# Six bundles of attention behind feed-forward blocks, and TensorE's queue in source order from unit 5 on

## The chip, the cores and the metric

The kernel runs on one core of a Trainium2 chip. A core has five engines with a queue each: TensorE (PE in the profile; its weight loads are listed apart as PEld), VectorE (DVE), ScalarE (ACT), GpSimd (POOL) and SyncE (SP), which here only issues DMA transfers. Each queue is executed in order; the engines run side by side and wait for one another through semaphores. The metric is the device time of one execution in microseconds (us); less is better.

## The reference

The program computes a gated linear attention and feeds its result to a feed-forward layer. All arrays are float32, with 4 batches, 8 heads, 768 tokens and head dimension 48.

```python
mag = np.sqrt(a_re * a_re + a_im * a_im)
scale = np.minimum(mag, 0.999) / (mag + 1e-06)
a_re_n, a_im_n = (a_re * scale, a_im * scale)
...
for t in range(S):
    ar, ai = (a_re_n[:, :, t, :, None], a_im_n[:, :, t, :, None])
    new_re = ar * S_re - ai * S_im
    new_im = ar * S_im + ai * S_re
    kv = np.einsum('bhd,bhe->bhde', k[:, :, t], v[:, :, t])
    S_re, S_im = (new_re + kv, new_im)
    y[:, :, t] = np.einsum('bhd,bhde->bhe', q[:, :, t], S_re)
...
x = np.ascontiguousarray(attn_out.transpose(0, 2, 1, 3)).reshape(B * S, H * D)
a = x @ w_a
b = x @ w_b
return (a * b @ w_out).astype(np.float32)
```

The state of each head is a complex 48x48 matrix that decays by its own complex factor per row at each token; the feed-forward has 3072 rows, 384 columns in and out, and 1536 columns inside.

## The kernel before

**Units.** The tokens are cut into chunks of 128, and a unit is one chunk of two batches: 256 columns of tokens. There are 12 units, 0 to 11 (`NU`): six chunks of the first pair of batches, then six of the second. Unit 6 starts from an empty state; units 5 and 11 are the last of their pair and need not update it.

**Three stages work on three units at once.** In the window of unit w (the loop `for w in range(NU)`), TensorE does the feed-forward of unit w and the attention of unit w+1, while DVE and ACT prepare unit w+2 and, late in the window, begin unit w+3.

- `prep(u)` (lines 203 to 337) turns the decay factors into products over the chunk and scales q and k by them. Its last operations are the two products of line 312 per unit, DVE operations of 1536 elements per partition, which write the buffer `qk`. It is a generator: the window's loop draws some of its operations after each block.
- `stack(u)` (line 342) then moves `qk` by ten DMA transfers from SP into the buffer `stk` (line 352), head by head. There is one `qk` and one `stk`: the next unit's `qk` is loaded when the stacking has read it, and `stk` is written anew when the attention of the unit before has read it.
- `attn(u)` does the attention, for each of the two batches i of the unit and each group g of four heads: `scores` (line 385, four float32 products of 128x128 per group from `stk` into a PSUM tile `pm`; DVE then masks them into `am`, line 388), `transposes` (line 396, the keys turned by TensorE into a `pm`, copied by ACT into `kt`, line 400), `outputs` (line 425, which adds `v`·`am` and state·`q` in an `xp` tile; its products use a 32-column strip of the array each, four side by side), ACT's copy of `xp` into `xh` (line 429), `residual` (line 434: DVE takes what the copy lost into `xl`), and `state` (line 442, `kt`·`v` into a `pm`; DVE adds it to the state, line 449, and rescales in some units, line 453). There are two `pm`, two `am` and two `kt` buffers and one `xp`.
- The feed-forward of a unit runs over 12 blocks f of 128 inner columns. `gemm1` (line 486) makes 18 products of 256 columns for a block in one of three PSUM tiles `ab`, from `xh` and `xl` and weights split into two parts; ACT and DVE multiply the two halves and split the result (lines 494 to 497). `gemm2` (line 504) makes six products of 384 columns for a block. It follows `gemm1` by two blocks (`LAG`): in the loop of block f stands `gemm1(f)`, then, through `second()`, `gemm2(f-2)`. All these use float32r, a one-pass format, on the full array.

**What sets the order.** The programming library records the instructions in the order of the source and a scheduler then fixes each engine's queue, ahead of the run, by priority (`tc.high_priority` raises it) and by its own estimate of when an operand is ready. So the source order of the attention pieces is a wish, which the scheduler may break up. On the chip the queues are fixed.

In window w the attention generator of unit w+1 yields after each of its 18 pieces (12 in units 5 and 11). `slot()` is called twice per block, behind `gemm1` and behind `gemm2`; from block `ATTN_AT` (5 for w = 0, 6 after) to block `STACK_AT` (11 for w = 0 to 2, 10 after) each call draws one or two pieces. At block `STACK_AT` what is left is drawn, `prep(w+2)` is finished, `stack(w+2)` is issued and the next `qk` is loaded.

Of the kernel before, what the change touches and what calls it, by code (L numbers as in the profile page):

```python
# [20 lines left out]
NCH = S // C  # L21
# [25 lines left out]
EARLY = 2  # L47
WARM = 8
HB = 3
O_BUFS = 3  # L50
CONV_ON_AB = 7
NCHK = NU * G + NU + 1
# [2 lines left out]
P1_AT = 4  # L55
MOE_FIRST = 4000
ATTN_FIRST = 2000
ATTN_AT = (5, 6, 6, 6, 6)
STACK_AT = (11, 11, 11, 10, 10)


# [9 lines left out]
def tile_kernel(ctx: ExitStack, tc: tile.TileContext, a_d, qk_d, v_d, w_d, qn_d, kn_d, vn_d, an_d, out_d):  # L71
    nc = tc.nc
    vec, act, pe, sync = nc.vector, nc.scalar, nc.tensor, nc.sync
# [57 lines left out]
    def split_weights():  # L131
        for f in range(NF):
            for m, (c0, n) in enumerate(WPART):
                raw = raws[f, m]
                t = moe.tile([128, n], F32, name="o_sb", bufs=O_BUFS)
                tu = t.bitcast(U32)
# [202 lines left out]
    def load_qk(u):  # L339
        sync.dma_start(out=qk[:, :, 1, 0:2 * TOK], in_=qk_d[u])  # L340

    def stack(u, cols=None):
        n = RUN if rescaled(u % NCH) else 2 * TOK
        if cols is None:
            cols = slice(TOK if u < EARLY else 0, n)
        for h in range(H):
            r0 = h * D
            while r0 < (h + 1) * D:
                j, p = divmod(r0, 128)
                m = min((h + 1) * D - r0, 128 - p)  # L350
                d0 = 2 * (r0 - h * D)
                sync.dma_start(out=stk[d0:d0 + 2 * m, h, cols], in_=qk[p:p + m, j, :, cols])
                r0 += m
# [4 lines left out]
    def load_v(u):  # L358
        for i in range(2):
            t = vpool.tile([128, 512], F32, name="v_t")  # L360
            sync.dma_start(out=t, in_=v_d[u, i])
            v_tiles[u, i] = t
# [8 lines left out]
    def attn(u, xh, xl):  # L371

        c = u % NCH
        last = c + 1 == NCH
# [61 lines left out]
        def state(i, hg):  # L436
# [10 lines left out]
            with tc.high_priority(offset=ATTN_FIRST):  # L447
# [4 lines left out]
                if rescaled(c):  # L452
                    vec.tensor_tensor(out=uv, in0=uv, in1=sv, op=ALU.mult)

        order = [(scores, 0, 0), (scores, 0, 1), (transposes, 0, 0), (transposes, 0, 1),
                 (outputs, 0, 0), (outputs, 0, 1), (scores, 1, 0), (residual, 0, 0), (state, 0, 0), (scores, 1, 1),
                 (state, 0, 1), (transposes, 1, 0), (transposes, 1, 1), (outputs, 1, 0),
                 (outputs, 1, 1), (state, 1, 0), (residual, 1, 0), (state, 1, 1)]
        if u == 0:
            order = [(scores, 0, 0), (scores, 0, 1), (outputs, 0, 0), (outputs, 0, 1), (scores, 1, 0), (scores, 1, 1),  # L460
                     (residual, 0, 0), (outputs, 1, 0), (outputs, 1, 1), (transposes, 0, 0), (transposes, 0, 1),
                     (residual, 1, 0), (state, 0, 0), (state, 0, 1), (transposes, 1, 0), (transposes, 1, 1),
                     (state, 1, 0), (state, 1, 1)]
        for fn, i, g in order:
            if not (last and fn in (transposes, state)):
                fn(i, g)
                yield

    def pieces(u):
        return 12 if u % NCH + 1 == NCH else 18  # L470

    def new_x():
        return (moe.tile([128, NJ, TOK], F32, name="xh"), moe.tile([128, NJ, TOK], F32, name="xl"))
# [6 lines left out]
    def gemm1(f, xh, xl, ps_ab=ps_ab, moe=moe):  # L480
        ab = ps_ab.tile([128, 512], F32, name="ab")
        for m in range(2):
            n = 0
            for i in range(NJ):
                for part, xt in ((0, xh), (0, xl), (1, xh)):
                    pe.matmul(out=ab[:, m * TOK:(m + 1) * TOK],  # L486
                              lhsT=r(w_ab(f, part, m * NJ + i)),
                              rhs=r(xt[:, i, :]), start=n == 0, stop=n == 8)
                    n += 1
        h_t = moe.tile([128, TOK], F32, name="h_t")  # L490
        hh = moe.tile([128, TOK], F32, name="hh", bufs=HB)
        hl = moe.tile([128, TOK], F32, name="hl", bufs=HB)
        with tc.high_priority(offset=MOE_FIRST):
            act.copy(out=h_t, in_=ab[:, 0:TOK])  # L494
            vec.tensor_tensor(out=h_t, in0=ab[:, TOK:2 * TOK], in1=h_t, op=ALU.mult)  # L495
            act.copy(out=r(hh), in_=h_t)  # L496
            vec.tensor_tensor(out=r(hl), in0=h_t, in1=hh, op=ALU.subtract)  # L497
        return hh, hl

    def gemm2(f, hh, hl, os_):  # L500
        for tt in range(2):
            ts = slice(tt * 128, (tt + 1) * 128)
            for n, (ht, part) in enumerate(((hh, 0), (hh, 1), (hl, 0))):
                pe.matmul(out=os_[tt][:, 0:DM], lhsT=r(ht[:, ts]), rhs=r(w_t[f, 2][:, part, :]),  # L504
                          start=(f == 0 and n == 0), stop=(f == NF - 1 and n == 2))
# [107 lines left out]
    def drain(gen, ns=None):  # L613
        if gen is None:
            return
        left = ns
        for cost in gen:
            if left is not None:
                left -= cost or 0
                if left <= 0:  # L620
                    return
# [10 lines left out]
    for _ in attn(0, *x_cur):  # L632
        drain(p1, P1_A)
    pend = []

    def second():
        w2, f2, hh, hl, os2 = pend.pop(0)
        gemm2(f2, hh, hl, os2)
        if f2 == NF - 1:
            for tt in range(2):  # L640
                o_sb = moe.tile([128, DM], F32, name="o_sb", bufs=O_BUFS)
                with tc.high_priority(offset=MOE_FIRST):
                    act.copy(out=o_sb, in_=os2[tt][:, 0:DM])
                act.dma_start(out=out_d[w2, tt], in_=o_sb)

    pgen = None
    for w in range(NU):
        last = w + 1 == NU
        x_nxt = None if last else new_x()
        at = None if last else attn(w + 1, *x_nxt)  # L650
        if not last:
            load_v(w + 1)
        os_ = [ps_o.tile([128, 512], F32, name=f"o{t}") for t in range(2)]
        slots = [0, 2 * (STACK_AT[min(w, 4)] + 1 - max(ATTN_AT[min(w, 4)], 0 if w else P1_AT + 1))]
        left = [pieces(w + 1)]

        def slot():
            if at is None or f < ATTN_AT[min(w, 4)] or (w == 0 and f <= P1_AT) or not slots[1]:
                return
            n = -(-left[0] // slots[1])  # L660
            slots[1] -= 1
            for _ in range(n):
                next(at, None)
                left[0] -= 1

        for f in range(NF):
            if w == 0:
                next(ws, None)
                drain(p1, P1_F)
                if f == P1_AT:  # L670
                    drain(p1)
                    stack(1)
                    for i in range(WARM):
                        wp = ps_m.tile([128, 512], F32, name="pm")
                        pe.matmul(out=wp[:, 0:TOK], lhsT=ident, rhs=qk[:, i % NJ, 1 - i // NJ % 2, TOK:2 * TOK],
                                  start=True, stop=True)
                    load_qk(2)
                    pgen = prep(2)
            pend.append((w, f, *gemm1(f, *x_cur), os_))
            slot()  # L680
            if len(pend) > LAG:
                second()
            slot()
            if f == STACK_AT[min(w, 4)]:
                drain(at)
                if w + 2 < NU:
                    drain(pgen)
                    stack(w + 2)
                if w + 3 < NU:
                    load_qk(w + 3)  # L690
                    pgen = prep(w + 3)
            if w > 0:
                drain(pgen, 2400)
        x_cur = x_nxt
# [8 lines left out]
    vec.tensor_scalar(out=bad, in0=tot[0:1, 0:1], scalar1=128.0 * NCHK, scalar2=None, op0=ALU.not_equal)  # L703
    while pend:
        second()
    fast.close()
    with tc.If(nc.values_load(bad[0:1, 0:1], min_val=0, max_val=1) > 0):
        token_by_token()
# [55 lines left out]
```

## Time and profile before

| | |
|---|---|
| time, median of 3 runs | 699.11 us (698.85 to 699.16) |
| time of the profiled execution | 698.89 us |
| its span, first to last instruction | 697.2 us |
| mean granted TensorE clock | 0.974 |
| PE, PEld, DVE, ACT busy | 655.2, 610.8, 551.8, 308.9 us |

The page of the profile lists busy time by engine, the span in 40 slices with a busy digit each (17.4 us a slice), the chain of work that ended last, and groups of instructions by line. Other views are a timeline of one engine (start, duration, engine, line, operation, tiles, shapes, count, and in brackets idle time and what ended it), the waits (who waited for whom: total, times, longest) and busy time by stretch. A float32 product is two MATMUL records in a timeline and one instruction in an order (a transpose and a float32r product are one in both). A record's duration covers its way through the array, so records overlap; what a stretch of work costs is the distance from its first start to the start of what follows.

Until about 120 us the weights are loaded and split and the first units prepared; the blocks of a window then follow one another to the end, about 51 us a window with attention in it.

### The profile page before, as it was taken

What the parts mean: (1) busy time and instruction counts of PE and PEld (TensorE: products, weight loads), DVE (VectorE), ACT (ScalarE), POOL (GpSimd) and SP (SyncE); (2) the same over time, 40 slices, a digit from 0 to 9 for tenths busy, and PEclk for the clock granted to TensorE, in tenths of its full rate; (3) what the DMA queues carried; (4) which work ended last, traced back from release to release, by engine and by line L of the source; (5) the groups of instructions that cost most, each with busy time, mean ns of one, the idle gap of its engine ahead of it and who ended that gap; (6) DMA issues with size and microseconds to landing.
All of it is one profiled execution on the core that took longest, in us unless ns stands there. A gap on an engine that the chain in (4) does not pass through costs nothing.

```text
span 697.2 us, 14316 instructions
## 1 busy us (share of the span) xinstructions
PE 655.2 (94%) x5854; PEld 610.8 (88%) x5854; DVE 551.8 (79%) x1241; ACT 308.9 (44%) x618; POOL 5.6 (1%) x11
## 2 busy tenths in 40 slices
PE   3557999999999999999999999999999999999996
PEld 1224889899899999999999999999999999999996
DVE  5999899988888889989899898999989853232221
ACT  6357755634535445245363554535542332221221
POOL 3000000000000000000000000000000000000000
PEclk9567999999999999999999999999999999999999
DMA  8973202411414205134151340511510500400000
GB/s 312 402 291 108 79 1 54 129 55 55 128 42 130 81 28 149 60 98 129 25 160 46 102 134 1 169 67 47 145 46 2 165 25 17 106 24 2 24 1 28
DMA packets 32088, 63.94 MB, mean 92 GB/s; under 512 B 3984, under 2 KB 10640, under 8 KB 32016
## 3 DMA queue, kind: packets, MB, share of 16 engines
q1 hardware_dynamic: 28560, 58.23, 27.0%
q10 hardware_dynamic: 3456, 4.72, 1.9%
q8 instruction: 48, 0.79, 0.5%
q14 instruction: 24, 0.20, 0.1%
HBM read 39.32 MB, written 4.72 MB: 63 GB/s over the span
## 4 chain that ended last, share of the span: by engine, by line
PE 64%; DVE 27%; ACT 4%; DMA 2%; issue 1%; SPq 1%; ACTq 0%; DVEq 0%
PE ab L486 30%; PE o L504 14%; PE xp L425 6%; PE pm L385 5%; PE pm L442 4%; DVE a_t L292 3%; DVE pr L230 2%; DVE qk L312 2%; DVE h_t L495 2%; PE pm L396 2%; DVE hl L497 2%; PE pm L150 2%; DVE z L297 2%; DVE pb L260 1%; DVE z L236 1%
## 5 line engine op out<-in xcount | busy, mean ns | idle before, releaser
L486 PE MATMUL ab<-xh,w 128*128 128x256 f32 x1728 | 339.0, 285 | 0.0
L486 PEld LDWEIGHTS ab<-xh,w 128*128 128x128 f32 x1728 | 278.1, 190 | 1.8 <-issue 1.4
L486 PE MATMUL ab<-xl,w 128*128 128x256 f32 x864 | 245.1, 284 | 0.0
L486 PEld LDWEIGHTS ab<-xl,w 128*128 128x128 f32 x864 | 164.4, 190 | 0.5 <-issue 0.2
L504 PE MATMUL o<-w,hh 128*128 128x384 f32 x576 | 152.3, 344 | 0.0
L494 ACT COPY h_t<-ab 128x256 f32<-128x256 f32 x144 | 53.1, 369 | 176.9 <-PE ab L486 176.8
L495 DVE TENSOR_TENSOR h_t<-ab,h_t 128x256 f32<-128x256 f32 x144 | 60.5, 420 | 72.5 <-ACT h_t L494 72.3
L504 PEld LDWEIGHTS o<-w,hh 128*128 128x128 f32 x576 | 96.8, 190 | 3.7 <-issue 3.0
L504 PE MATMUL o<-w,hl 128*128 128x384 f32 x288 | 96.9, 336 | 0.0
L496 ACT CAST hh<-h_t 128x256 fp32r<-128x256 f32 x144 | 58.0, 403 | 81.1 <-DVE h_t L495 80.9
L497 DVE TENSOR_TENSOR hl<-h_t,hh 128x256 fp32r<-128x256 f32 x144 | 60.5, 420 | 17.5 <-ACT hh L496 17.3
L150 PE MATMUL ab<-o_sb,ident 128*128 128x384 f32 x42 | 29.1, 794 | 29.9 <-DVE o_sb L141 29.8
L385 PE MATMUL pm<-stk 128*128 128x128 f32 x384 | 54.4, 279 | 2.7 <-DMA stk<-qk 2.7
L504 PEld LDWEIGHTS o<-w,hl 128*128 128x128 f32 x288 | 54.1, 188 | 0.0
L385 PEld LDWEIGHTS pm<-stk 128*128 128x128 f32 x384 | 48.7, 191 | 5.9 <-issue 4.8
L230 DVE TENSOR_TENSOR pr<-z 128x384 f32<-128x384 f32 (+1 forms) x91 | 47.1, 524 | 2.4 <-ACT z L216 0.8
L150 PEld LDWEIGHTS ab<-o_sb,ident 128*128 128x128 f32 x42 | 10.2, 286 | 39.8 <-DVE o_sb L141 29.4
L292 DVE TENSOR_TENSOR a_t<-z,b_t 128x768 f32<-128x768 f32 x48 | 44.6, 952 | 0.1
L425 PE MATMUL xp<-am,v_t 128*32 128x128 f32 x768 | 42.5, 277 | 1.3 <-DVE am L388 1.2
L312 DVE TENSOR_TENSOR qk<-qk,z 128x1536 f32<-128x1536 f32 (+1 forms) x28 | 42.7, 1524 | 0.1
L388 DVE TENSOR_TENSOR am<-pm,mask 128x512 f32<-128x512 f32 x48 | 32.8, 685 | 5.0 <-PE pm L385 4.8
L425 PE MATMUL xp<-stk,u 128*32 128x128 f32 x640 | 34.4, 273 | 0.0
(106 smaller groups left out, 761.7 us busy)
## 6 DMA issues: line engine op xcount, KB each, us to landing
w<-in_dram SPq DMA_DIRECT2D x36, 384.0 KB, 8.1
qk<-in_dram SPq DMA_DIRECT2D x12, 768.0 KB, 4.8
a_t<-in_dram SPq DMA_DIRECT2D x11, 768.0 KB, 4.3
stk<-qk SPq DMA_DIRECT2D x42, 192.0 KB, 3.3
v_t<-in_dram SPq DMA_DIRECT2D x24, 256.0 KB, 2.7
out_dram<-o_sb ACTq DMA_DIRECT2D x24, 192.0 KB, 1.9
stk<-qk SPq DMA_DIRECT2D x18, 192.8 KB, 3.4
stk<-qk SPq DMA_DIRECT2D x14, 128.0 KB, 3.1
```

Of the source, the lines that this page charges most:

```text
L150: pe.matmul(out=lp[:, 0:n], lhsT=ident, rhs=t, start=True, stop=False)
L230: vec.tensor_tensor(out=pr[:, :, :, o:o + n], in0=view(zz, W + at_(i) + 2 * o, [[W, 2], [-W, 2], [2, n]]), in1=tok(slice(1, 3), i - 1, o, ...
L292: vec.tensor_tensor(out=pz[:, s].rearrange("p (j b e) -> p j b e", j=SUB // 2, e=2), in0=zb[:, 1 + s], in1=view(bb, (1 + k - s) * NB, [[0, ...
L312: vec.tensor_tensor(out=qk4[:, :, k, x0:x1], in0=qk4[:, :, 1, x0:x1], in1=z[:, k].rearrange("p (j t) -> p j t", j=NJ).unsqueeze(2).broadca ...
L385: pe.matmul(out=sp[:, h4], lhsT=stk[:, h, ks], rhs=stk[:, h, qs], start=True, stop=True)
L425: pe.matmul(out=xp[qd * 32:(qd + 1) * 32, ti], lhsT=l, rhs=rr, start=st, stop=sp_, tile_position=(0, qd * 32), skip_group_check=True)
L486: pe.matmul(out=ab[:, m * TOK:(m + 1) * TOK], lhsT=r(w_ab(f, part, m * NJ + i)), rhs=r(xt[:, i, :]), start=n == 0, stop=n == 8)
L494: act.copy(out=h_t, in_=ab[:, 0:TOK])
L495: vec.tensor_tensor(out=h_t, in0=ab[:, TOK:2 * TOK], in1=h_t, op=ALU.mult)
L496: act.copy(out=r(hh), in_=h_t)
L497: vec.tensor_tensor(out=r(hl), in0=h_t, in1=hh, op=ALU.subtract)
L504: pe.matmul(out=os_[tt][:, 0:DM], lhsT=r(ht[:, ts]), rhs=r(w_t[f, 2][:, part, :]), start=(f == 0 and n == 0), stop=(f == NF - 1 and n == 2))
```

## The change

The attention generator of units 1 to 11 now issues whole kinds together and yields six times (three in units 5 and 11, which have no transposes and no state):

1. both scores of batch 0
2. both transposes of batch 0
3. both halves of the outputs of batch 0, both scores of batch 1, the residual of batch 0
4. both states of batch 0
5. both transposes of batch 1
6. both halves of the outputs of batch 1, its residual, both its states

`slot()` is called once per block, behind `gemm2`, and draws one bundle at the blocks of `at_f`: 6 to 11 for w = 0 to 2, 5 to 10 from w = 3 on, and 6, 8 and 10 for the windows w = 4 and 10. Unit 0 keeps its order. From window w = 4 on (`w + 1 == LED`) to the end of the feed-forward a manual schedule holds for TensorE: its queue is then exactly the source order; the other engines' queues, and TensorE's before that, are still the scheduler's. `STACK_AT` and all sizes and buffers stay.

```diff
+LED = 5
...
-ATTN_AT = (5, 6, 6, 6, 6)
 STACK_AT = (11, 11, 11, 10, 10)
...
-        order = [(scores, 0, 0), (scores, 0, 1), (transposes, 0, 0), (transposes, 0, 1),
-                 (outputs, 0, 0), (outputs, 0, 1), (scores, 1, 0), (residual, 0, 0), (state, 0, 0), (scores, 1, 1),
-                 (state, 0, 1), (transposes, 1, 0), (transposes, 1, 1), (outputs, 1, 0),
-                 (outputs, 1, 1), (state, 1, 0), (residual, 1, 0), (state, 1, 1)]
...
-        for fn, i, g in order:
-            if not (last and fn in (transposes, state)):
-                fn(i, g)
-                yield
+        if u > 0:
+            order = [(scores, 0, 0), (scores, 0, 1), None, (transposes, 0, 0), (transposes, 0, 1), None,
+                     (outputs, 0, 0), (outputs, 0, 1), (scores, 1, 0), (scores, 1, 1), (residual, 0, 0), None,
+                     (state, 0, 0), (state, 0, 1), None, (transposes, 1, 0), (transposes, 1, 1), None,
+                     (outputs, 1, 0), (outputs, 1, 1), (residual, 1, 0), (state, 1, 0), (state, 1, 1), None]
+        given = 0
+        for piece in order:
+            if piece is None:
+                if given:
+                    yield
+                given = 0
+            elif not (last and piece[0] in (transposes, state)):
+                piece[0](*piece[1:])
+                given += 1
+                if u == 0:
+                    yield
 
     def pieces(u):
-        return 12 if u % NCH + 1 == NCH else 18
+        return 3 if u % NCH + 1 == NCH else 6
...
     pgen = None
+    ordered = ExitStack()
     for w in range(NU):
...
-        slots = [0, 2 * (STACK_AT[min(w, 4)] + 1 - max(ATTN_AT[min(w, 4)], 0 if w else P1_AT + 1))]
-        left = [pieces(w + 1)]
+        n_b = 0 if last else pieces(w + 1)
+        at_f = [STACK_AT[min(w, 4)] - 6 // n_b * k for k in range(n_b)]
+        if w + 1 == LED:
+            ordered.enter_context(tc.manual_schedule(engines={pe.engine}))
 
         def slot():
-            if at is None or f < ATTN_AT[min(w, 4)] or (w == 0 and f <= P1_AT) or not slots[1]:
-                return
-            n = -(-left[0] // slots[1])
-            slots[1] -= 1
-            for _ in range(n):
+            if f in at_f:
                 next(at, None)
-                left[0] -= 1
...
             pend.append((w, f, *gemm1(f, *x_cur), os_))
-            slot()
             if len(pend) > LAG:
                 second()
             slot()
...
     while pend:
         second()
+    ordered.close()
     fast.close()
```

Three places in TensorE's queue follow. Line numbers of the changed kernel are 8 higher behind `attn` (L494 and L512 are the `gemm1` and `gemm2` of L486 and L504); names that end in numbers are weights (`w_`) and the two output tiles (`o_`).

The first is the outputs of batch 1 of unit 6 (units 4 to 11 are alike, with `xp<-stk,u` rows between the `xp<-am,v_t` rows), before:

```order
L396 MATMUL pm<-ident,stk 128x96 x4
L425 MATMUL xp<-am,v_t 32x128 x8
L504 MATMUL o_4189<-w_847,hh 128x384 x2
L504 MATMUL o_4189<-w_847,hl 128x384
L504 MATMUL o_4190<-w_847,hh 128x384 x2
L504 MATMUL o_4190<-w_847,hl 128x384
L425 MATMUL xp<-am,v_t 32x128 x8
L442 MATMUL pm<-v_t,kt 96x48 x4
L486 MATMUL ab<-xh,w_1011 128x256
```

and in the changed kernel:

```order
L512 MATMUL o_4191<-w_905,hh 128x384 x2
L512 MATMUL o_4191<-w_905,hl 128x384
L512 MATMUL o_4192<-w_905,hh 128x384 x2
L512 MATMUL o_4192<-w_905,hl 128x384
L425 MATMUL xp<-am,v_t 32x128 x16
L442 MATMUL pm<-v_t,kt 96x48 x8
L494 MATMUL ab<-xh,w_1100 128x256
```

The two halves of the outputs stand together, one block later than before, and both states behind them. Counted over the queue, TensorE comes to line 425 from another kind of work 4, 7, 5 and 3 times in units 1 to 4 before, and 3, 4, 2 and 2 times now; in each of units 5 to 11 it is 3 times before and 2 times now. Transposes are begun 3 times in a unit of the later windows before and 2 times now, states 4 times and 2 times.

The second is the step from the scores to the transposes of batch 0 of unit 7, before:

```order
L486 MATMUL ab<-xh,w_757 128x256
L385 MATMUL pm<-stk 128x128 x8
L504 MATMUL o_4814<-w_482,hh 128x384 x2
L504 MATMUL o_4814<-w_482,hl 128x384
L504 MATMUL o_4815<-w_482,hh 128x384 x2
L504 MATMUL o_4815<-w_482,hl 128x384
L396 MATMUL pm<-ident,stk 128x96 x8
L486 MATMUL ab<-xh,w_827 128x256
```

and now (the scores first, and what follows them):

```order
L512 MATMUL o_4816<-w_452,hl 128x384
L512 MATMUL o_4817<-w_452,hh 128x384 x2
L512 MATMUL o_4817<-w_452,hl 128x384
L385 MATMUL pm<-stk 128x128 x8
L494 MATMUL ab<-xh,w_747 128x256
```

The scores stand ahead of the `gemm1` of block 6 instead of behind it, and between them and the transposes there are now a whole `gemm1` and a `gemm2`, where there was a `gemm2` alone.

The third is the start of unit 4's attention, in window 3, where the scheduler still sets the queue. Before, the first five heads' scores stand behind the whole of `gemm1` of block 6:

```order
L486 MATMUL ab<-xh,w_757 128x256 x2
L486 MATMUL ab<-xl,w_757 128x256
L486 MATMUL ab<-xh,w_757 128x256
L385 MATMUL pm<-stk 128x128 x5
L504 MATMUL o_2926<-w_482,hh 128x384 x2
```

and now the first two stand ahead of it and a third one inside it:

```order
L512 MATMUL o_2927<-w_452,hl 128x384
L385 MATMUL pm<-stk 128x128 x2
L494 MATMUL ab<-xh,w_747 128x256
L494 MATMUL ab<-xl,w_747 128x256
L494 MATMUL ab<-xh,w_747 128x256 x2
L494 MATMUL ab<-xl,w_747 128x256
L494 MATMUL ab<-xh,w_747 128x256 x2
L494 MATMUL ab<-xl,w_747 128x256
L385 MATMUL pm<-stk 128x128
```

On DVE the operations that stand ahead of each unit's last product of line 312 are the same in number and kind up to unit 4, and differ by one or two operations of the feed-forward or the attention later. SP's queue is the same but for one load of `v_t` that moves by one place.

## The prediction

> **What bounds the kernel now.** I read the page first, then the stretches.
>
> ```profile
> PE 655.2 (94%) x5854; PEld 610.8 (88%) x5854; DVE 551.8 (79%) x1241; ACT 308.9 (44%) x618; POOL 5.6 (1%) x11
> PE   3557999999999999999999999999999999999996
> DVE  5999899988888889989899898999989853232221
> ```
>
> TensorE is full from slice 8 (140 us) to the end. But a busy record is not peak, so what counts is what a stretch costs from start to start. DVE falls to 2 tenths in the last sixth, and TensorE keeps its pace there.
>
> ```profile
> 173.70:223.00 49.30, 46.71 (x450) 43.71 (x448) 43.06 (x94) 23.98 (x45) 0.00 (x0) 1.00 0.31 93
> 274.00:325.00 51.00, 50.91 (x499) 49.57 (x498) 47.49 (x103) 26.67 (x50) 0.00 (x0) 1.00 0.36 106
> 476.00:527.00 51.00, 50.93 (x498) 49.43 (x496) 46.84 (x98) 23.40 (x45) 0.00 (x0) 1.00 0.28 81
> 578.00:629.00 51.00, 51.00 (x527) 49.63 (x529) 14.94 (x34) 12.74 (x32) 0.00 (x0) 1.00 0.18 50
> ```
>
> The columns are length, then busy time of PE, PEld, DVE, ACT and POOL, the granted clock, and DMA. A window takes 51 us with DVE at 46.84 and with DVE at 14.94: TensorE's own queue sets it, at full clock. The exception is early:
>
> ```profile
> 173.72 0.28 PE L486 MATMUL ab<-xh,w 128*128 128x256 f32 x1
> 175.66 0.46 PE L385 MATMUL pm<-stk 128*128 128x128 f32 x2 [1.66 <-DMA stk<-qk]
> 221.73 0.34 PE L504 MATMUL o<-w,hl 128*128 128x384 f32 x1
> 223.08 0.46 PE L385 MATMUL pm<-stk 128*128 128x128 f32 x2 [1.00 <-DMA stk<-qk]
> 217.85 1.67 DVE qk L312
> 219.55 3.39 DMA stk<-qk
> ```
>
> The scores of units 2 and 3 stand for the stacking, and the chain of waits (the last two rows) shows it follows DVE's last product of line 312 at once. Up to unit 3 DVE sets the pace.
>
> **The change part by part.** *A: fewer visits to the outputs.* Inside the window after 476 us:
>
> ```profile
> 478.86 0.43 PE L425 MATMUL xp<-am,v_t 128*32 128x128 f32 x8
> 480.75 0.62 PE L504 MATMUL o<-w,hh 128*128 128x384 f32 x2
> 481.92 1.05 PE L385 MATMUL pm<-stk 128*128 128x128 f32 x8
> 491.19 0.42 PE L425 MATMUL xp<-am,v_t 128*32 128x128 f32 x8
> 492.21 0.62 PE L504 MATMUL o<-w,hh 128*128 128x384 f32 x2
> 493.46 0.43 PE L425 MATMUL xp<-am,v_t 128*32 128x128 f32 x8
> 494.47 0.88 PE L442 MATMUL pm<-v_t,kt 128*96 128x48 f32 x8
> 504.50 0.51 PE L504 MATMUL o<-w,hh 128*128 128x384 f32 x2
> 505.55 0.28 PE L486 MATMUL ab<-xh,w 128*128 128x256 f32 x1
> ```
>
> Batch 0's 64 records in one visit take 478.86 to 480.75, 1.89 us; batch 1's in two take 1.02 and 1.01, 2.03 us: 0.14 more. The `gemm2` between plain work takes 1.05 (504.50 to 505.55), behind a visit 1.17 (480.75 to 481.92), and between two visits 1.25 (492.21 to 493.46): 0.20 more. So one visit more costs 0.14 + 0.20 = 0.34 us. Units 4 to 11 lose one visit each: 8 x 0.34 = 2.7 us. All of it lies on TensorE, where nothing else runs meanwhile.
>
> [...]
>
> *B: fewer visits to the other kinds.*
>
> ```profile
> 488.24 0.51 PE L396 MATMUL pm<-ident,stk 96*128 96x96 f32 x4
> 488.54 0.36 PE L486 MATMUL ab<-xh,w 128*128 128x256 f32 x1
> 490.77 0.50 PE L396 MATMUL pm<-ident,stk 96*128 96x96 f32 x4
> 502.35 0.28 PE L486 MATMUL ab<-xh,w 128*128 128x256 f32 x1
> ```
>
> A `gemm1` behind four transposes takes 488.54 to 490.77, 2.23 us, against 2.15 (502.35 to 504.50). The last transpose is still under way when the `gemm1` starts (four of them span 0.51, the next start comes after 0.30), so some of the 0.08 is the transposes' own time, and a visit costs between nothing and 0.08. Three visits fewer (one of transposes, two of states) in six of these units, 18: between 0 and 1.4 us. I take 0.03 each, 0.5 us, near the lower end, because that overlap of 0.21 is more than the 0.08.
>
> *C: transposes that stood for DVE.* From 230 to 640 us the waits list
>
> ```profile
> PEld pm L396 <- DVE am L388: 1.8, 4, 0.7
> PEld xp L425 <- DVE am L388: 1.1, 3, 0.6
> PE pm L396 <- DVE am L388: 0.7, 2, 0.4
> 474.88 1.28 DVE L388 TENSOR_TENSOR am<-pm,mask 128x512 f32<-128x512 f32 x2
> ```
>
> Scores fill both `pm` tiles; the transposes need them back, and DVE's two masks take 1.28 us. Only a `gemm2` (1.05 us) covers that now. In the changed order a whole block does, 2.15 + 1.05 = 3.2 us. The outputs come two blocks behind their scores. The waits overlap in these rows: TensorE itself idled at least 0.7, the loads 2.9 together. I take 2.0 us, nearer the loads' figure, since a held load holds its product.
>
> *D: units 1 to 3.* They lose 1, 3 and 3 visits, 7 x 0.34 = 2.4 us, ahead of unit 4. What units 1 and 2 save, the next scores wait longer for the stacking (175.66 and 223.08 stay), because DVE's queue has the same operations ahead of line 312. Unit 3's 1.0 us meets this:
>
> ```profile
> 271.98 0.28 PE L486 MATMUL ab<-xh,w 128*128 128x256 f32 x1
> 274.13 1.27 PE L385 MATMUL pm<-stk 128*128 128x128 f32 x10
> 267.84 6.64 SPq L352 DMA_DIRECT2D stk<-qk  x10
> stk<-qk SPq DMA_DIRECT2D x42, 192.0 KB, 3.3
> 354.19 6.75 SPq L352 DMA_DIRECT2D stk<-qk  x10
> 372.27 1.78 PE pm L385 x16
> ```
>
> Unit 4's scores move ahead of the `gemm1` at 271.98, which TensorE would now reach at 271.0. The ten transfers are issued over 6.64 us from 267.84 and land 3.3 later: the first head at 271.1, the second 0.7 later at 271.8. So the two moved scores stand up to 0.8 us. The gain left is between nothing and 1.0, and at most the 1.4 of units 1 and 2 on top, if DVE too waits less for TensorE and stacks earlier. I take 0.4, within the first. SP's queue is passed unchanged but for one load of `v_t`.
>
> Unit 6's scores move ahead by 2.15 too. Its stacking, issued from 354.19 over 6.75 us, lands by 354.19 + 6.75 + 3.3 = 364.2; the scores came at 372.27 and now, with 2 us gained by then, come near 368: covered by some 4 us.
>
> *E: new waits.* In source order nothing passes a bundle whose tiles are late; behind it stand the next `gemm1`, and behind that ACT's and DVE's lines 494 to 497. At the five handovers of a unit the cover is one block, 3.2 us. The longest work of DVE that can stand ahead of what TensorE needs is
>
> ```profile
> 479.74 1.76 DVE L312 TENSOR_TENSOR qk<-qk,z 128x1536 f32<-128x1536 f32 x1
> 483.42 0.42 DVE L497 TENSOR_TENSOR hl<-h_t,hh 128x256 fp32r<-128x256 f32 x1
> 483.75 0.55 DVE L434 TENSOR_TENSOR xl<-xp,xh 128x384 fp32r<-128x384 f32 x1
> 481.75 1.75 DVE L312 TENSOR_TENSOR qk<-qk,z 128x1536 f32<-128x1536 f32 x1
> ```
>
> two of line 312 around a line 497: 1.76 + 0.42 + 1.75 = 3.9, over the cover by 0.7. Bounds: nothing, and 0.7 in each of eight units, 5.6. I take one such overrun, 0.7, since today's waits with a third of the cover are 0.7 at most. The next unit's first `gemm1` needs `xl` of batch 1, and stands behind the outputs by a block and two states, over 3.2 us; DVE's line 434 takes 0.55 and ACT's copy of the same tile, as an estimate from it, as much: covered.
>
> **Sum.** Gain 2.7 + 0.5 + 2.0 + 0.4 - 0.7 = 4.9 us. Before is the profiled 698.89, so 694.0; the median of the runs is 699.11, 0.2 above it, and I predict 694.2 us.
>
> **The rivals.**
>
> *DVE becomes the bound* in units 4 to 8. In 274 to 325 us it is busy 47.49 of 51.00, and if the other 3.5 can't be had either, TensorE only waits longer, and gains stay in units 9 to 11, where DVE thins out: 3 x (0.34 + 0.09) + 0.5 of C = 1.8, time 697.3. For it: it is so up to unit 3. Against it: unit 6's stacking is done some 8 us ahead of its scores, so DVE runs ahead.
>
> *The cost stays.* If the 0.34 belongs to what stands beside the outputs and not to a visit, scores and states beside them pay as `gemm2` did, A is nothing, and E eats C: 698.9. Against it: 1.89 against 2.03 is inside the outputs alone.
>
> *Strict order holds TensorE, slower.* One mechanism: at one handover a unit, DVE is a product of line 312 (1.75 us) later than the block covers, because the scheduler sets DVE's queue by its own estimate and TensorE no longer does something else. Eight units: 14.0, less A, B and D's 3.6: 698.9 + 10.4 = 709.3. It decides from 0.6 us a unit, where gain and loss cancel. For it: both `pm` tiles go to one bundle, so every next bundle depends on DVE or ACT; the waits of C are of this kind. Against it: three times the cover.
>
> [...]
>
> **How the numbers follow.** Forecast 0.68 (own range 692.0 to 696.5), DVE the bound 0.12, cost stays 0.08, strict order slower 0.12. A difference of 0.2%, 1.4 us, is about what a measurement of this kernel tells from no change. DVE the bound, at 1.6 us, counts to faster by 0.11 and to same by 0.01. Faster 0.79, same 0.09, slower 0.12. At their best bounds B, C, D and E would add 0.9 + 0.9 + 2.0 + 0.7 = 4.5, hardly all at once: the range goes down by 2.7, to 691.5. Its upper end takes in the cases without gain: 699.2, leaving the strict-order case out.
>
> **What would show it.** A: in units 4 to 11 two stretches of line 425 of about 1.89 us each, none of 1.0, and windows shorter by about 0.4 each even in 578 to 629 us, where DVE does little. B: hardly to be seen. C: no wait of line 396 for line 388. D: waits for the stacking longer at units 2 and 3, a short one at unit 4. E: a wait at a bundle's head or at a `gemm1` for line 388, 400, 434 or 449. Wrong would be: the stretch behind unit 4 not shorter by 3 us or more, or TensorE idle there for over 2 us in all.

## The result, and the profile after

The changed kernel takes 691.41 us (median of 4 runs, 691.05 to 692.08), the kernel before 698.98 (4 runs, 698.72 to 699.16): a ratio of 0.9895, 95% interval 0.9879 to 0.991. That is 7.6 us less, where 4.9 were forecast; the time lies below the forecast and just below 691.5, the lower end of its range. The profiled execution is the slowest of the four, 692.08 us, with a span of 690.4.

The page of the kernel after, busy time and two rows of the slices:

```profile
PE 647.5 (94%) x5854; PEld 607.9 (88%) x5854; DVE 552.1 (80%) x1241; ACT 306.7 (44%) x618; POOL 5.6 (1%) x11
...
PE   3647999999999999999999999999999999999996
DVE  6999899998898979989899898999989963233221
```

TensorE does the same 5854 records in 7.7 us less, and DVE's total has not moved (551.8 before): TensorE is the bound as it was. Busy time by stretch, after, in the window of unit 6 and in that of unit 10 (columns as in the prediction):

```profile
403.20:453.70 50.50, 50.50 (x499) 49.26 (x498) 47.81 (x104) 26.58 (x50) 0.00 (x0) 1.00 0.36 104
605.30:651.30 46.00, 46.00 (x449) 45.10 (x449) 14.09 (x30) 11.12 (x28) 0.00 (x0) 1.00 0.03 9
```

TensorE's records fill both, with DVE at 47.81 and at 14.09.

Where the time went shows when each window's first `gemm2` starts, read from the two timelines:

| | before | after | lead of after |
|---|---|---|---|
| window 0 | 88.4 | 88.0 | 0.4 |
| window 1 | 153.5 | 152.8 | 0.7 |
| window 3 | 261.4 | 258.1 | 3.3 |
| window 4 | 312.2 | 308.6 | 3.6 |
| window 8 | 510.9 | 504.0 | 6.9 |
| window 11 | 658.8 | 651.3 | 7.5 |
| last product starts | 690.8 | 683.4 | 7.4 |

The attention of unit u stands in window u - 1. The 0.4 at the start of window 0 stands ahead of all attention of units 1 to 11, and I take it as the difference of two executions. So units 1 to 3 brought 2.9 us, and units 4 to 11 another 4.1. Not every window got shorter: window 9, in 578 to 629 us of the kernel before, where about 0.4 less was forecast, takes 51.03 us after (554.22 to 605.26, first `gemm2` to first `gemm2`) against 50.55 before (561.80 to 612.35), because of the second of the waits below.

TensorE's timeline in window 7 of the kernel after, all of line 425 and what follows it:

```profile
464.29 1.95 PE L385 MATMUL pm<-stk 128*128 128x128 f32 x16
465.99 0.36 PE L494 MATMUL ab<-xh,w 128*128 128x256 f32 x1
...
473.25 0.42 PE L425 MATMUL xp<-am,v_t 128*32 128x128 f32 x8
475.13 2.05 PE L385 MATMUL pm<-stk 128*128 128x128 f32 x16
476.94 0.36 PE L494 MATMUL ab<-xh,w 128*128 128x256 f32 x1
...
488.94 0.43 PE L425 MATMUL xp<-am,v_t 128*32 128x128 f32 x8
490.82 1.56 PE L442 MATMUL pm<-v_t,kt 128*96 128x48 f32 x16
```

There are two visits of 1.88 us each (473.25 to 475.13, 488.94 to 490.82), as forecast. The scores behind a visit take 1.81 (475.13 to 476.94), those behind a `gemm2` 1.70 (464.29 to 465.99): they pay 0.11 for their place, which the prediction did not count.

TensorE's waits from 125 to 690 us, after:

```profile
PE pm L385 <- DMA stk<-qk: 2.2, 2, 1.6
PE o L512 <- ACT o_sb L651: 0.5, 1, 0.5
PE ab L494 <- DVE xl L434: 0.2, 1, 0.2
```

The waits for masks (line 388) are gone. Beside the stacking two short ones are left; the longer is the first `gemm2` of window 9, whose second half waits for ACT's copy of the finished output:

```profile
555.46 0.61 PE L512 MATMUL o<-w,hh 128*128 128x384 f32 x2 [0.55 <-ACT o_sb L651]
```

### The profile page after: what moved, and what is told of

Read it like the earlier page. It is cut to its first block, busy times and chain, and to the rows that moved or that the text cites. A ratio compares the mean times of both kernels' runs of the same rounds, so it can differ in the third digit from the quotient of the medians.

```text
span 690.4 us, 14307 instructions
## 1 busy us (share of the span) xinstructions
PE 647.5 (94%) x5854; PEld 607.9 (88%) x5854; DVE 552.1 (80%) x1241; ACT 306.7 (44%) x618; POOL 5.6 (1%) x11
## 4 chain that ended last, share of the span: by engine, by line
PE 59%; DVE 31%; ACT 4%; DMA 2%; issue 2%; SPq 0%; ACTq 0%; DVEq 0%
PE ab L494 28%; PE o L512 13%; PE pm L385 5%; PE xp L425 4%; DVE a_t L292 3%; DVE qk L312 3%; PE pm L442 3%; DVE pr L230 2%; DVE hl L505 2%; DVE h_t L503 2%; PE pm L150 2%; DVE z L297 2%; DVE pb L260 2%; DVE z L236 1%; PE ab L150 1%
## 5 line engine op out<-in xcount | busy, mean ns | idle before, releaser
L494 PE MATMUL ab<-xh,w 128*128 128x256 f32 x1728 | 339.5, 285 | 0.0
L494 PEld LDWEIGHTS ab<-xh,w 128*128 128x128 f32 x1728 | 278.0, 190 | 1.0 <-issue 0.6
L494 PE MATMUL ab<-xl,w 128*128 128x256 f32 x864 | 245.1, 284 | 0.2 <-DVE xl L434 0.2
L494 PEld LDWEIGHTS ab<-xl,w 128*128 128x128 f32 x864 | 164.5, 190 | 1.0 <-DVE xl L434 0.7
L512 PE MATMUL o<-w,hh 128*128 128x384 f32 x576 | 149.5, 338 | 0.5 <-ACT o_sb L651 0.5
L504 ACT CAST hh<-h_t 128x256 fp32r<-128x256 f32 x144 | 58.2, 404 | 100.4 <-DVE h_t L503 100.0
L512 PEld LDWEIGHTS o<-w,hh 128*128 128x128 f32 x576 | 97.2, 190 | 1.7 <-ACT o_sb L651 1.1
L512 PE MATMUL o<-w,hl 128*128 128x384 f32 x288 | 97.0, 337 | 0.0
L512 PEld LDWEIGHTS o<-w,hl 128*128 128x128 f32 x288 | 54.1, 188 | 0.0
L425 PE MATMUL xp<-am,v_t 128*32 128x128 f32 x768 | 39.7, 276 | 0.7 <-DVE am L388 0.6
L425 PE MATMUL xp<-stk,u 128*32 128x128 f32 x640 | 32.7, 273 | 0.0
```

The lines of the kernel that those rows point to most:

```text
L425: pe.matmul(out=xp[qd * 32:(qd + 1) * 32, ti], lhsT=l, rhs=rr, start=st, stop=sp_, tile_position=(0, qd * 32), skip_group_check=True)
L494: pe.matmul(out=ab[:, m * TOK:(m + 1) * TOK], lhsT=r(w_ab(f, part, m * NJ + i)), rhs=r(xt[:, i, :]), start=n == 0, stop=n == 8)
```

## Experiments

"After" is the changed kernel. Each ratio is to the kernel before, measured along with it (698.94 us for the first four, 699.07 for the next four, 699.04, and 698.46 for the last two). The lengths of windows run from first `gemm2` to first `gemm2` in the one profiled execution of each kernel; the attention in window w is that of unit w + 1:

| window | before | after | `late` | `split_late` | `no_cover` |
|---|---|---|---|---|---|
| 4 | 47.08 | 46.07 | 47.00 | 46.40 | 46.07 |
| 5 | 48.94 | 48.53 | 48.55 | 49.06 | 52.45 |
| 6 | 51.24 | 50.42 | 50.21 | 51.62 | 51.93 |
| 7 | 51.38 | 50.36 | 50.21 | 51.09 | 51.97 |
| 8 | 50.91 | 50.21 | 50.21 | 52.89 | 51.93 |
| 9 | 50.55 | 51.03 | 50.29 | 51.09 | 50.87 |
| 10 | 46.40 | 46.07 | 46.07 | 46.40 | 46.07 |

**1 and 2: the change in the late units alone, and in the early units alone.** `late` bundles units 5 to 11 and keeps the source order there; units 1 to 4 have the 18 pieces and their places as before. `early` bundles units 1 to 4, with the scheduler throughout.

```diff
+    def bundled(u):
+        return u >= 5
...
-            if f in at_f:
...
+            if bundled(w + 1):
+                if f in at_f:
+                    next(at, None)
+                return
...
```

In `early` the condition is `0 < u < 5`, and `LED` is 99.

> Bundles and source order for units 5 to 11 alone; units 1 to 4 keep their 18 single pieces and the scheduler's queue. If the gain of the two halves adds up as the two traces say (TensorE was 3.6 us ahead at the first gemm2 of window 4 and 7.4 us at the end), this keeps the late 3.8 and loses the early 3.6: 695.2 us. If the late part needs the early one (TensorE arrives earlier and then only waits longer for the stacking), about 697. If the early lead is nothing but a different start of that one profiled execution, 691.8.

> Bundles for units 1 to 4 alone; units 5 to 11 keep single pieces, and the scheduler sets TensorE's queue to the end. Adding up: 699.0 less the early 3.6 = 695.4 us. If the early lead is lost again behind unit 4, where TensorE would stand for the stacking, about 698.5. If all of the gain came from the early part, 691.4.

Measured: `late` 694.92 us (694.15 to 695.88), ratio 0.9938 (0.9925 to 0.9951), 4.0 less; `early` 696.63 us (695.66 to 696.97), ratio 0.9967 (0.9954 to 0.998), 2.3 less. Both parts gain, and the sum of 6.3 comes near the whole. What is missing is lost at the border, in window 4, the attention of unit 5: it takes 46.07 us after, but 47.00 in `late` and 47.93 in `early`, where unit 5 gets four visits and this wait (300 to 690 us; line 389 of that kernel is the masks, line 426 the outputs):

```profile
PE xp L426 <- DVE am L389: 0.9, 1, 0.9
```

`early` also bundles unit 4, whose window is only 0.2 shorter in it than before; its windows 0 to 2, with units 1 to 3, are 2.9 shorter. That speaks against the 0.4 of step D.

**3 and 4: the visits alone, given back.** The changed kernel, but the two halves of each batch's outputs are parted by one piece of scores or state, in units 5 to 11 (`split_late`) or 1 to 3 (`split_early`). In both, the second half of batch 1's outputs reads a state that is already renewed for the first four heads; the work is the same in amount. The lines with a minus show the order of after, those with a plus the order of these units.

```diff
-                     (outputs, 0, 0), (outputs, 0, 1), (scores, 1, 0), (scores, 1, 1), (residual, 0, 0), None,
+                     (outputs, 0, 0), (scores, 1, 0), (outputs, 0, 1), (scores, 1, 1), (residual, 0, 0), None,
...
-                     (outputs, 1, 0), (outputs, 1, 1), (residual, 1, 0), (state, 1, 0), (state, 1, 1), None]
+                     (outputs, 1, 0), (state, 1, 0), (outputs, 1, 1), (residual, 1, 0), (state, 1, 1), None]
```

> The changed kernel, but in units 5 to 11 the two halves of the outputs are parted by one score (batch 0) or one state (batch 1). TensorE comes to the outputs 12 times more in these units (3, 4, 4, 4, 4, 4, 3 visits where it was 2), and no operation is added. If a visit costs 0.34 us, as the prediction had it, 691.4 + 4.1 = 695.5 us. If the cost belonged to the neighbours beside the outputs and not to the visit, or were hidden, 691.4 to 692.0.

> The changed kernel, but in units 1 to 3 the halves are parted in the same way: 6, 7 and 5 visits to the outputs where it was 3, 4 and 2, 9 more. If the early gain, 3.6 us where 0.4 was forecast, is the visits saved on TensorE there, they cost 9 x 0.34 = 3.1 us: 694.5 us. If DVE sets the pace up to unit 4 and ran earlier because it stood less for TensorE, the visits themselves are mostly swallowed and DVE's queue decides: 691.4 to 692.6, with the stacking of unit 4 issued within 1 us of the changed kernel's 265.1.

Measured: `split_late` 698.8 us (697.49 to 700.71), ratio 1.0 (0.999 to 1.0011), with 12 visits more; that is 7.4 more than after, beyond both of the times expected. TensorE's timeline of it, batch 0 of one unit:

```profile
424.27 0.43 PE L425 MATMUL xp<-am,v_t 128*32 128x128 f32 x8
...
425.28 1.16 PE L385 MATMUL pm<-stk 128*128 128x128 f32 x8
426.37 0.43 PE L425 MATMUL xp<-am,v_t 128*32 128x128 f32 x8
...
427.38 1.16 PE L385 MATMUL pm<-stk 128*128 128x128 f32 x8
428.30 0.36 PE L499 MATMUL ab<-xh,w 128*128 128x256 f32 x1
```

The same products that after does in 3.69 us (473.25 to 476.94) take 4.03 here (424.27 to 428.30). Nothing waits in between, so one visit costs 0.34 beside scores, as it did beside `gemm2` before. The table says the same: units 5 and 11, in windows 4 and 10, have one visit more than in after and take 0.33 more each. Twelve visits make 4.1. The rest of the loss is not visits: the parted outputs of batch 1 now wait for DVE's renewal of the state (line 453):

```profile
PE xp L425 <- DVE u L453: 2.1, 2, 1.7
```

The two, 6.2 us, account for the 6.0 by which its profiled execution (698.10) is longer than that of after (692.08); the median of its 12 executions lies 0.7 above that one, and no trace shows what they spend it on.

`split_early` took 694.85 us (694.79 to 695.44), ratio 0.9942 (0.993 to 0.9955): 3.4 more than after for nine visits more, 3.1 at 0.34 each; its windows 0 to 2 are 2.8 longer than those of after. So what is lost ahead of the stage that DVE paces is not swallowed there. How it passes through shows SP's queue, the ten transfers of a stacking (start, length), for units 2 to 4. Before:

```profile
172.18 6.66 SPq L352 DMA_DIRECT2D stk<-qk  x10
219.55 6.66 SPq L352 DMA_DIRECT2D stk<-qk  x10
267.84 6.64 SPq L352 DMA_DIRECT2D stk<-qk  x10
```

After:

```profile
171.17 6.63 SPq L352 DMA_DIRECT2D stk<-qk  x10
217.76 6.67 SPq L352 DMA_DIRECT2D stk<-qk  x10
265.09 6.67 SPq L352 DMA_DIRECT2D stk<-qk  x10
```

`split_early`:

```profile
171.93 7.68 SPq L352 DMA_DIRECT2D stk<-qk  x10
219.38 6.63 SPq L352 DMA_DIRECT2D stk<-qk  x10
267.16 6.76 SPq L352 DMA_DIRECT2D stk<-qk  x10
```

The stackings come 1.0, 1.8 and 2.8 us earlier after the change (0.4 of each from the start), and 0.8, 1.6 and 2.1 of that is lost again in `split_early`. DVE's chain to the stacking is not fixed: DVE's own waits from 122 to 268 us show why. Before:

```profile
DVE am L388 <- PE pm L385: 3.2, 5, 0.9
...
DVE u L449 <- PE pm L442: 1.3, 4, 0.3
```

After:

```profile
DVE am L388 <- PE pm L385: 2.2, 3, 0.9
...
DVE u L449 <- PE pm L442: 0.6, 2, 0.4
```

DVE stands for TensorE's scores and states 4.5 us before and 2.8 after; the waits for ACT in the same two lists add up to 10.1 and 9.8. The operations for masks and states stand in DVE's queue ahead of line 312, so what TensorE does sooner, DVE does sooner. That is 1.7 of the 2.4 by which unit 4's stacking gained on the start. In `split_early` DVE stands 3.4 for scores and states, and beside that

```profile
DVE u L449 <- PE xp L425: 1.2, 2, 0.7
DVE am L388 <- PE xp L425: 0.5, 1, 0.5
```

These two are waits for the parted outputs themselves, which hold a state and a mask here and in neither of the other kernels. So `split_early` shows that time lost ahead of this stage comes out at the end, but it does not part the price of the visits from what the new order does to DVE.

**5: the bundles without the order of the source.** `free` is the changed kernel with the scheduler throughout.

```diff
-LED = 5
+LED = 99
```

> The six bundles as in the change, but the scheduler sets TensorE's queue throughout (the number LED is 99 instead of 5). Theory V (the gain is fewer visits to the column-tiled outputs and transposes out of reach of the masks, and the bundles do both by themselves): the visits per unit are 6, 3, 4 and then 2 as in the changed kernel, so 691.4 again, within 0.8. Rival O (the order of the source is itself worth something from unit 5 on, since the scheduler would move pieces forward into waits): some of the waits of attention pieces for masks come back, 0.3 to 1.0 in each of the windows 4 to 10, and the time is 693.5 to 698.

Measured: 691.65 us (691.41 to 691.92), ratio 0.9894 (0.988 to 0.9909). The visits per unit are those of after, and so is the time: with bundles, the order of the source is worth nothing that these runs can tell.

**6: the order of the source without the bundles.** `strict` has the 18 pieces and their places as before, and source order from unit 5 on.

```diff
+    def bundled(u):
+        return u == 0
```

> The 18 single pieces and their places as in the kernel before, but TensorE's queue in the order of the source from unit 5 on. Visits per unit stay 6, 4, 7, 5 and then 3. Theory V: without fewer visits nothing is gained from them; the waits of transposes for masks (0.2 to 0.4 a unit) may go or grow, since two pieces stand at one place and a piece must now wait where the scheduler would have let the feed-forward pass: 697.5 to 703. Rival O (the order of the source carries the late gain): 695, as the kernel with bundles and order from unit 5 on (694.92).

Measured: 701.95 us (700.25 to 702.38), ratio 1.0038 (1.0026 to 1.005): 2.9 slower than before. Its waits from 300 us on:

```profile
PE pm L397 <- DVE am L389: 2.9, 4, 1.7
PE xp L426 <- DVE am L389: 0.3, 1, 0.3
```

The kernel before has 0.7 and 0.3 in these two rows, so 2.2 of the 2.9 are waits for masks. Rival O falls on both sides. The rival "strict order holds TensorE" is real, but at pieces that stand half a block apart, not at bundles with a block between them.

**7: the cover taken away.** `no_cover` is after, but in units 6 to 10 the transposes of batch 0 stand right behind its scores; the five bundles that are left begin one block later.

```diff
-            order = [(scores, 0, 0), (scores, 0, 1), None, (transposes, 0, 0), (transposes, 0, 1), None,
+            order = [(scores, 0, 0), (scores, 0, 1), (transposes, 0, 0), (transposes, 0, 1), None, None,
...
+        if w + 1 > LED and n_b == 6:
+            at_f = at_f[:5]
```

> The changed kernel, but in units 5 to 10 the transposes of batch 0 stand in the same bundle right behind its scores, so that nothing covers the two masks between them; the transposes need the scores' two PSUM tiles. Visits to the outputs stay 2 per unit. Theory C1: TensorE stands for VectorE's two masks each time, by the mask's own durations and its place in VectorE's queue 1 to 2 us, in six units (unit 5's second batch has none): 691.4 + 5 to 6 x 1.5 = 699 to 700. Theory C2: the wait is only what the kernel before showed at that place, 0.2 to 0.5 per unit, since VectorE comes to the first mask while the second scores run: 693.0 to 694.0.

Measured: 699.91 us (698.45 to 701.97), ratio 1.0015 (1.0005 to 1.0024): 8.5 more than after, with the outputs' visits unchanged. By the table windows 6 to 8 each take 1.5 to 1.7 more, window 5 takes 3.9 more, and window 9, in which DVE does little, no more than after, or 0.6 more than in `late`, which has no wait in it. The waits of it from 125 us on:

```profile
PE pm L396 <- DVE am L388: 4.7, 6, 1.7
...
PE pm L396 <- ACT kt L400: 1.5, 2, 1.0
```

6.2 us stand there; some of the rest is a slower clock in window 5 (0.64 and 0.93 in two stretches of 4 us, below), so that C1's number is met in part by luck. Its mechanism holds: one block between scores and transposes hides the whole wait.

**8 to 11: one visit per unit.** If a visit costs 0.34, both batches' outputs should stand together. `one_visit` does so with a second tile for the outputs, one `ab` tile fewer and fewer buffers elsewhere:

```diff
+            order = [(scores, 0, 0), (scores, 0, 1), None, (scores, 1, 0), (scores, 1, 1), None,
+                     (transposes, 0, 0), (transposes, 0, 1), None,
+                     (outputs, 0, 0), (outputs, 0, 1), (outputs, 1, 0), (outputs, 1, 1),
+                     (residual, 0, 0), (residual, 1, 0), (state, 0, 0), (state, 0, 1), None,
+                     (transposes, 1, 0), (transposes, 1, 1), None, (state, 1, 0), (state, 1, 1), None]
```

> A try at a better version: both batches' outputs stand in one bundle (scores 0; scores 1; transposes 0; all four halves of the outputs, both residuals and states 0; transposes 1; states 1), for which the outputs get two PSUM tiles and the feed-forward's first product two instead of three, the masks' results four buffers instead of two, and the feed-forward's h_t, hh and hl and the output's o_sb one buffer fewer each. Visits per unit 6, 3, 5 and then 1, so 9 fewer from unit 3 on and one more in unit 2. Theory V at 0.33 a visit: 691.4 - 8 x 0.33 = 688.7. Rival W (with one buffer fewer at each of these places the feed-forward waits for VectorE and ScalarE in its blocks, 144 of them): with 0.05 to 0.1 us more in each of 144 blocks 695 to 703.

Measured: 693.91 us (693.57 to 694.95), ratio 0.9933 (0.992 to 0.9945): 2.5 more than after. That is between the two theories. The loss is not in the blocks, as rival W had it: window 6 takes 49.9 us against 50.4 after, but window 0 takes 68.6 against 64.9. TensorE's waits in it come to 1.5 us; the longest is the weights' conversion, which stands for DVE, and where the rest of the 3.7 goes is not shown:

```profile
122.89 0.59 PE L150 MATMUL pm<-o_sb,ident 128*128 128x384 f32 x1 [0.98 <-DVE o_sb L141]
```

`one_better` leaves those buffers alone: batch 1's outputs borrow one of the three `ab` tiles, `kt` and `am` share four buffers, and transposes 0 follow the outputs.

```diff
+                xps[i] = (ps_ab.tile([128, 512], F32, name="ab")[:, 0:NJ * C].rearrange("p (j t) -> p j t", j=NJ)
+                          if u > 0 and i == 1 else ps_x.tile([128, NJ, C], F32, name="xp"))
```

> The second try at one visit per unit, without taking buffers from the first windows: six bundles (scores 0; scores 1; all four halves of the outputs, both residuals, transposes 0; states 0; transposes 1; states 1), the second batch's outputs in a PSUM tile of the feed-forward's three instead of one of its own, the keys turned (kt) and the masked scores (am) in one set of four buffers, h_t with one buffer instead of two. Visits per unit from unit 1 on: one at least fewer in each. Theory V at 0.33 to 0.34 a visit: nine to eleven fewer, 3.0 to 3.7, so 687.7 to 688.4, and 687.2 if the one wait of 0.55 at 554.58 goes too. Rival W (the first try's loss came with one visit itself and not from window 0, where its trace shows 3.8 of longer window; or the one tile that the outputs borrow holds gemm1): 690.5 to 694.

Measured: 691.53 us (690.77 to 692.35), ratio 0.9899 (0.9881 to 0.9917), no better than after. Window 0 takes 71.3 us here, 6.5 more than after; windows 1 and 2 win 5.3 of that back. The cause, as far as the queue shows it, is another one: the borrowed tile is next in turn after outputs that come late, so the scheduler can no longer put `gemm1` ahead of them, and TensorE stands (line 682 is the `WARM` products in front of unit 1's attention):

```profile
117.84 0.54 PE L151 MATMUL pm<-w,nident 128*128 128x384 f32 x1
121.98 1.65 PE L682 MATMUL pm<-qk,ident 128*128 128x256 f32 x3 [3.60 <-DVE qk L312]
```

A second loss is in window 4, 1.4 us longer than after, with a wait of 0.96 for line 435 (the residual). The last two begin with unit 3 and with unit 2 (`u >= 3`, `u >= 2` in place of `u > 0`).

> As the second try at one visit per unit, but only from unit 3 on; units 1 and 2 keep the changed kernel's bundles and the outputs' own PSUM tile, so that window 0 has the changed kernel's order (in the second try TensorE stood 3.60 at 118 there, since the borrowed tile was given to outputs that came late). Theory V: one visit fewer in each of units 3 to 11, 9 x 0.335 = 3.0 from 691.4: 688.4, and 687.9 without the wait at 554.58. Rival W (single visits give their gain back in other waits, as the second try's windows 4 and 7 with 0.96 and 0.40): 690 to 692.

> The same from unit 2 on, where the stacking is still waited for. Theory V: one or more visits fewer there too: 688.0. Rival W (the late stacking of unit 2 holds the borrowed tile, and through it gemm1): a longer wait in window 1 than the 1.57 and 0.17 of the changed kernel, 689 to 691.

Measured: `one_from_3` 689.12 us (688.64 to 689.9), ratio 0.9866 (0.985 to 0.9882); `one_from_2` 688.73 us (687.7 to 689.52), ratio 0.9854 (0.9836 to 0.9871). Both beat after by more than 2 us and lie between their two theories; which of the two is better the intervals leave open. In window 10, which has no wait in either, `one_from_3` takes 45.73 us against 46.07 after: 0.34 for the one visit saved. `one_from_2`'s window 6 by stretch:

```profile
402.50:452.40 49.90, 49.90 (x498) 49.24 (x497) 46.37 (x103) 23.57 (x47) 0.00 (x0) 1.00 0.32 99
```

This is 49.90 against 50.50 in the row of after above: a visit and a little more. Some of its gain goes into new waits in window 1, as its rival W said; in the list from 125 us on:

```profile
PE pm L385 <- DVE am L388: 1.7, 2, 1.2
```

## Why the prediction was right, and where it was wrong

- **A, fewer visits to the outputs in units 4 to 11: right in its mechanism and nearly in its size.** 0.34 a visit, worked out from one window, is what a visit costs when it is put back alone (4.03 against 3.69). The rival "cost stays" falls as a whole: the products beside the outputs are the same in both, only parted or not. A grain of it is true, since the scores behind a visit pay 0.11.
- **B, fewer visits to the other kinds: nothing to be seen.** Where no mask is waited for, A and B can be read together: window 9 is 0.26 shorter in `late` than before (50.55 to 50.29), and window 10, where unit 11 has no transposes and states, 0.33. The prediction had 0.43 and 0.34. For the eight units that makes some 2.2 us, where 2.7 + 0.5 were forecast.
- **C, waits for masks: right, and larger than forecast.** No wait of line 396 for line 388 is left, and without the block between them it comes back at 1.5 to 1.7 a unit in windows 6 to 8. In `late`, windows 6 to 8 are 2.9 shorter than before, of which A and B, at 0.26 each, are 0.8; that leaves 2.1 in three windows. With 0.7 in window 4 (after) and 0.1 in window 5, worked out in the same way, it is some 2.9 as an estimate, where 2.0 was taken of the loads' 2.9.
- **E, new waits: size about right, place wrong.** It is not a bundle's head in the late windows but, at 555.46, a `gemm2` that waits 0.55 for ACT's copy of the last output, which the list of possible waits did not name, and 0.17 for line 434 in window 1. Window 9 of after is 0.74 longer than that of `late`, which has no such wait there, against the 0.7 that was taken; windows 6 and 7 are 0.4 longer together.
- **The sum over units 4 to 11: near, with some luck.** Forecast were 2.7 + 0.5 + 2.0 - 0.7 = 4.5 us, measured 4.1. A and B were set too high, by about as much as C was set too low.
- **D, units 1 to 3: wrong, and nearly the whole of the error.** It was set at 0.4 of its 2.4 and measured 2.9, 2.5 more; the whole gain was 2.7 more than forecast (in the medians). The step that failed: "What units 1 and 2 save, the next scores wait longer for the stacking, because DVE's queue has the same operations ahead of line 312." The operations are the same, but some of them stood for TensorE, and the stackings came earlier, by 2.8 us at unit 4 (0.4 of it from the start). The waits for the stacking, forecast to grow, went from 1.66 and 1.00 to:

```profile
174.59 0.46 PE L385 MATMUL pm<-stk 128*128 128x128 f32 x2 [1.57 <-DMA stk<-qk]
...
221.25 0.46 PE L385 MATMUL pm<-stk 128*128 128x128 f32 x2 [0.68 <-DMA stk<-qk]
```

  Unit 4's scores found the heads that they needed landed, without the forecast wait of up to 0.8. The seven visits at 0.34 make 2.4, and the two waits for the stacking are 0.4 shorter together; that adds up to about the 2.9, though no run parts it further. The prediction had named this way, "if DVE too waits less for TensorE", and counted it as a bound instead of reading DVE's waits, where the 3.2 and the 1.3 stood.
- **The rivals.** DVE did not become the bound in units 4 to 8: it is busy 47.81 of 50.50 in window 6, and that window shrank by 0.8. Strict order held TensorE only without bundles (experiment 6). In experiment 7, where the transposes need the two `pm` tiles that the scores have just filled, 8.5 us were lost, the slower clock included; with one block between, no such wait is left.

## What to carry to other kernels

When products of a few columns of the array stand between full ones, count how often the queue enters them, price one entry by the same products parted and unparted (0.34 us here), and put them together; then put what needs the freed tiles one block later, and not in the same place (8.5 us in `no_cover`, its slower clock included). Before a gain ahead of a stage that another engine paces is written off, look at that engine's own waits: if it stands there for the engine that gets faster, the gain can go through, as the 2.9 us of units 1 to 3 did here. And a buffer that is borrowed or cut for a late stage must be followed into the first windows, where it cost `one_visit` 3.7 us and `one_better` 6.5, of which 5.3 came back.

## What was not expected of the hardware

Behind two stands of TensorE, 1.66 and 0.37 us, the granted clock was 0.64 in `no_cover`; behind one of 1.65 in `strict` it was 1.00. In `no_cover`, window 5, TensorE's timeline:

```profile
372.12 0.55 PE L396 MATMUL pm<-ident,stk 96*128 96x96 f32 x4 [1.66 <-DVE am L388]
373.04 0.84 PE L396 MATMUL pm<-ident,stk 96*128 96x96 f32 x4 [0.37 <-DVE am L388]
373.59 0.56 PE L499 MATMUL ab<-xh,w 128*128 128x256 f32 x1
377.13 0.52 PE L517 MATMUL o<-w,hh 128*128 128x384 f32 x2
```

Its busy time in the two stretches behind:

```profile
372.00:376.00 4.00, 3.51 (x19) 3.33 (x20) 3.90 (x15) 1.56 (x4) 0.00 (x0) 0.64 0.01 4
376.00:380.00 4.00, 4.00 (x53) 3.55 (x52) 2.93 (x7) 1.26 (x3) 0.00 (x0) 0.93 0.00 0
```

The granted clock is 0.64 and 0.93 there (1.00 in the 4 us ahead), and the `gemm1` takes 3.54 us (373.59 to 377.13) where one behind transposes took 2.23 before. In `strict`, the stand of 1.65 and the stretch behind it, whose clock is 1.00:

```profile
529.14 1.15 PE L397 MATMUL pm<-ident,stk 96*128 96x96 f32 x8 [1.65 <-DVE am L389]
```

```profile
530.00:534.00 4.00, 4.00 (x82) 3.87 (x84) 3.73 (x8) 2.21 (x5) 0.00 (x0) 1.00 0.00 0
```

That the stands are what lowered the clock in `no_cover` is not shown; what sets the two cases apart is open.
